# Three new planning margins and a longer one in a block-sparse attention and bilinear feed-forward kernel

## The chip, the cores and the metric

The kernel runs on one core of a Trainium2 chip. The metric is the device time in microseconds (us). The engines are TensorE (PE, with its weight loads PEld), VectorE (DVE), ScalarE (ACT), GpSimd (POOL) and SyncE (SP, which here only issues DMAs). All work in order: an instruction that waits holds up all that stand behind it on its engine.

## The reference

Four batches of eight heads attend over 768 positions of width 64. Positions are cut into 24 blocks of 32; a block of queries sees its neighbours, block 0, block 23 and three sampled blocks, and blocks 0 and 23 see everything:

```python
scores = scale * np.matmul(q, k.transpose(0, 1, 3, 2))
scores = np.where(mask, scores, -1000000000.0)
scores = scores - np.max(scores, axis=-1, keepdims=True)
attn = np.exp(scores)
attn = attn / (np.sum(attn, axis=-1, keepdims=True) + 1e-09)
x = np.matmul(attn, v)      # then heads side by side: 3072 rows of 512
out = ((x @ w_a) * (x @ w_b)) @ w_out   # 512 -> 1536 -> 512
```

Everything is float32; the kernel splits each operand into a high and a low float16 part, so that most products are three matmuls.

## The kernel before, in words

The attention goes by units, one block of queries of all heads: 96 units in 4 batches, 8 units to a chunk of 256 positions, 12 chunks. A sparse unit gathers its keys on POOL (lines 629 to 634, KG), computes scores on PE (L930, L1031), takes the maximum on DVE (L1046), exponentials on ACT (L1056), splits the weights (L948, L951, L955), turns them (on PE, L1109, for units 0 to 15; else by a DMA, L1081), and multiplies by gathered values (VG, loaded by SP at lines 656 to 669) on PE (L974). The sums go into xT (L1241, L1244). Eight finished units release one chunk of the feed-forward: 12 tiles of first products (L1273, "ab", 24 matmuls), their product on ACT and DVE (L1290 to L1305), 12 tiles of second products (L1333 to L1335).

A batch is prepared by `keys` and `values`: ACT's queue loads the raw tile (L493, L563), ACT takes its bound (L503, L571), POOL reduces it over partitions (L392), ACT and DVE make both halves (L508, L509; L583, L584). Keys are turned by PE in batch 0 (L541) and by a DMA in the others (L522); values are stored to memory (L588). `queries` loads a chunk's queries (L693), splits them (L704, L709, L711) and copies each half to the other partitions by a DMA (`turn_queries`, L735). The weights of the feed-forward come in 36 loads (L755), are rebuilt by DVE (L775 to L782) and split (L806 to L816); their raw tiles lie where the keys of batch 1 go later.

The order of all this is not written out. `Plan` keeps a clock of its own: each step of a flow yields an engine and a duration, and the plan takes next what can start first. An event carries the time at which it fired, and a flow that waits for it is not ready before. A plain number that is yielded moves a flow's ready time on by so much:

```python
if isinstance(got, int):
    self.ready += got
    value = self.ready
```

So a margin (LATE_Q, LATE_KS, LATE_VG and others) makes the plan believe that a DMA lands later. It adds no instruction and no wait to the program; it only moves what depends on that DMA, and with it everything else, to other places in the engines' orders. The rings of buffers are planned in the same way. Each DMA also takes one of eight landing counters in turn, whatever queue it is on, and its issuer waits until the DMA that had the counter before has landed; in the rows of the order below these are DMAHW0 to DMAHW7.

Of the kernel before, what the change touches and what calls it, by code (L numbers as in the profile page):

```python
# [53 lines left out]

LATE_PT, LATE_VG, LATE_AV, LATE_G = 2500, 2500, 1500, 700
LATE_S = 1000
LATE_HL, LATE_KS, LATE_Q = 2500, 2500, 2000
DMA_AHEAD = 1750
X_HIGH, X_UNITS = 600, 16

# [168 lines left out]
def dve(ns, fn):  # L229
    return [Way("DVE", ns, fn)]  # L230


def act(ns, fn):
    return [Way("ACT", ns, fn)]
# [6 lines left out]
def load_way(moved, fn):  # L241

    return [Way("LOAD", 475, fn, moved)]


def sp(ns, moved, fn):
    return [Way("SP", ns, fn, moved)]
# [3 lines left out]
def kernel(  # L251
# [41 lines left out]
    def take(tag, bufs):  # L293
        return rings.setdefault(tag, Ring(bufs)).take()
# [56 lines left out]
    v_stored = [Event(NG) for _ in range(B)]  # L351
    q_ready = [Event(3) for _ in range(NC)]
# [37 lines left out]
    def set_scale(a, floor=FLOOR):  # L390
        bits = power[:, a].bitcast(I32)
        yield pool(480, lambda: nc.gpsimd.partition_all_reduce(  # L392
            power[:, a], bound[:, a], P, bass_isa.ReduceOp.absmax
        ))
        yield dve(150, lambda: nc.vector.tensor_scalar(
            bits, bits, 0x7F800000, None, ALU.bitwise_and
        ))
        yield dve(150, lambda: nc.vector.tensor_scalar(
            rscale[:, a], power[:, a], floor, float(2.0 ** -14), ALU.max, ALU.mult
        ))  # L400
        end = yield dve(160, lambda: nc.vector.reciprocal(scale[:, a], rscale[:, a]))
        return end
# [67 lines left out]
    def gate(i):  # L470
        if i >= 0:
            yield s_sent[units[i]]

    def raw_tile(b, g, n):

        if b == 0:
            late = wab[:, NF // 2 :].rearrange("p f i a c x -> p (f i a c x)").bitcast(F32)
            late = late.rearrange("p (g x) -> p g x", x=2 * NT * D)
            return late[:, n * NG + g], parked
        yield w_freed  # L480
        t = stage[:, raw_taken[0] % RAW_BUFS]
        raw_taken[0] += 1
        freed = yield from take("raw", RAW_BUFS)
        return t, freed
# [5 lines left out]
    def keys(b, g):  # L490
        yield from gate(first_of[b] - GATE_KV)
        raw, freed = yield from raw_tile(b, g, 0)
        yield load_way(1000, lambda: nc.scalar.dma_start(raw, k[b, g]))  # L493
        if g + 1 < NG:
            plan.start(keys(b, g + 1), first_of[b] - LEAD_K)
        elif b > 0:
            plan.start(values(b, 0), first_of[b] - LEAD_V)
        t = raw.rearrange("p (t d) -> p t d", d=D)
        done = yield from take("ks", KS_BUFS)
        ks = work.tile([P, 2 * NT, P], F16, tag="ks", name=f"ks{b}_{g}", bufs=KS_BUFS)  # L500
        at = at_k + b * NG + g
        s = scale[:, at : at + 1]
        yield act(1020, lambda: nc.scalar.activation(  # L503
            ks[:, :, :D], t, AF.Abs, accum_out=bound[:, at : at + 1]
        ))
        end = yield from set_scale(slice(at, at + 1), FLOOR_QK)
        k_scale[b].fire(end)
        yield act(930, lambda: nc.scalar.activation(ks[:, :, :D], t, AF.Copy, scale=s))  # L508
        end = yield dve(1070, lambda: nc.vector.scalar_tensor_tensor(  # L509
            ks[:, :, D:], t, s, ks[:, :, :D], ALU.mult, ALU.subtract  # L510
        ))
        freed.fire(end)
        if b == 0:
            ends = Event(2)
            for h in range(2):
                plan.start(turn_keys(g, h, ks, ends, done), first_of[b] - LEAD_K, end)
            return
        if b == 1:
            yield w_freed
        if b >= 2:  # L520
            yield k_free[b - 2]
        end = yield sp(1700, 2200, lambda: nc.sync.dma_start_transpose(  # L522
            keysT[b % 2][:, 2 * g : 2 * g + 2, :].rearrange("p h (t s) -> p (h t) s", s=P),
            ks.rearrange("p t d -> p (t d)"),
        ))
        done.fire(end + LATE_KS)
        k_ready[b].fire(end + LATE_KS)
# [31 lines left out]
    def values(b, g):  # L559

        yield from gate(first_of[b] - GATE_KV)
        raw, freed = yield from raw_tile(b, g, 1)
        yield load_way(1000, lambda: nc.scalar.dma_start(raw, v[b, g]))  # L563
        if g + 1 < NG:
            plan.start(values(b, g + 1), first_of[b] - LEAD_V)
        elif b + 1 < B:
            plan.start(keys(b + 1, 0), first_of[b + 1] - LEAD_K)
        t = raw.rearrange("p (t x) -> p t x", t=NT)
        done = yield from take("ks", KS_BUFS)
        spare = work.tile([P, 2 * NT, P], F16, tag="ks", name=f"va{b}_{g}", bufs=KS_BUFS)  # L570
        end = yield act(1020, lambda: nc.scalar.activation(  # L571
            spare[:, :NT], t, AF.Abs,
            accum_out=bound_v[:, b * NG + g : b * NG + g + 1],
        ))
        done.fire(end)
        v_bound[b].fire(end)
        if g == NG - 1:
            plan.start(values_scale(b), first_of[b] - LEAD_V)
        yield v_scale[b]
        done = yield from take("ks", KS_BUFS)  # L580
        vs = work.tile([P, NT, 2, 2 * D], F16, tag="ks", name=f"vs{b}_{g}", bufs=KS_BUFS)
        s = scale[:, at_v + b : at_v + b + 1]
        yield act(930, lambda: nc.scalar.activation(vs[:, :, 0], t, AF.Copy, scale=s))  # L583
        end = yield dve(1015, lambda: nc.vector.scalar_tensor_tensor(  # L584
            vs[:, :, 1], t, s, vs[:, :, 0], ALU.mult, ALU.subtract
        ))
        freed.fire(end)
        end = yield sp(650, 1350, lambda: nc.sync.dma_start(  # L588
            vd[b][:, g * 4 * D : (g + 1) * 4 * D].rearrange("(t p) x -> p t x", p=P),
            vs.rearrange("p t a x -> p t (a x)"),  # L590
        ))
        done.fire(end)
        v_stored[b].fire(end)

    def values_scale(b):
        yield v_bound[b]
        at = at_v + b
        yield dve(150, lambda: nc.vector.reduce_max(
            bound[:, at : at + 1], bound_v[:, b * NG : (b + 1) * NG],
            axis=mybir.AxisListType.X,  # L600
        ))
        end = yield from set_scale(slice(at, at + 1))
        v_scale[b].fire(end)
# [79 lines left out]
    def queries(cc):  # L683
# [29 lines left out]
        ))  # L713
        freed.fire(end)
        plan.start(turn_queries(cc, 1), u0 - LEAD_Q, end)
        yield k_scale[b]

# [15 lines left out]
    def turn_queries(cc, a):  # L733

        end = yield sp(650, 700, lambda: nc.sync.dma_start(  # L735
            QT[cc][D:, 1 - a], QT[cc][:D, a]
        ))
        q_ready[cc].fire(end)


    def raw_weights(n, count):
# [722 lines left out]
```

## Time and profile before

| what | value |
|---|---|
| median of 3 runs | 862.08 us (860.63 to 865.51) |
| the profiled execution's own time | 856.35 us |
| its span, first to last instruction | 854.6 us |
| PE busy | 763.1 us, 89% |
| DVE busy | 587.0 us, 69% |
| ACT busy | 501.3 us, 59% |

Up to about 160 us the weights and the first batch are prepared while the first two chunks are attended to: DVE is nearly always busy there and PE is not. After it PE is busy nearly all the time, and from about 713 us on only feed-forward tiles are left. The page gives busy time over the whole span; the rows below are from views of single stretches.

### The profile page before, as it was taken

Reading aid. Unit: us, or ns where it says so; the run is one execution under the profiler, and the core shown is the slowest. Engines: PE = TensorE matmul, PEld = TensorE weight load, DVE = VectorE, ACT = ScalarE, POOL = GpSimd, SP = SyncE. Lnnn points to the kernel's source line nnn. Section 1 sums busy time; section 2 is a strip of 40 time slices with the busy share of each in tenths; the row PEclk is TensorE's granted clock in tenths of the full one; section 3 lists DMA queues with packets and bytes.
Section 4 is the critical chain, followed back from the end, with each engine's and each line's share of the span. In section 5 each row is a group of like instructions: output and inputs, shape, how many; then the busy total and the mean of one; then the engine's idle time right before and its main releaser. Section 6 shows DMA issues by size and latency. Waiting matters only on the chain.

```text
span 854.6 us, 24181 instructions
## 1 busy us (share of the span) xinstructions
PE 763.1 (89%) x9192; PEld 568.3 (66%) x9192; DVE 587.0 (69%) x1589; ACT 501.3 (59%) x1158; POOL 179.5 (21%) x428
## 2 busy tenths in 40 slices
PE   2256478799999979999999999999999999999998
PEld 1134366577767757767777867777777677777775
DVE  4999989998687568775677786755767876332222
ACT  6688779776675467684475765843845663232222
POOL 0642332300043133120034240200422310000000
PEclk9985589999999999999999999999999999999999
DMA  8767795577957589987676989667677767500000
GB/s 270 227 192 238 237 237 183 156 145 180 203 150 173 123 189 236 187 191 174 151 184 150 177 208 226 149 180 165 158 164 152 146 147 150 129 25 2 26 1 25
DMA packets 187758, 136.89 MB, mean 160 GB/s; under 512 B 130681, under 2 KB 155258, under 8 KB 187642
## 3 DMA queue, kind: packets, MB, share of 16 engines
q1 hardware_dynamic: 175712, 97.56, 51.7%
q10 hardware_dynamic: 11930, 37.79, 14.5%
q8 instruction: 72, 1.18, 0.6%
q14 instruction: 44, 0.36, 0.1%
HBM read 86.28 MB, written 12.58 MB: 116 GB/s over the span
## 4 chain that ended last, share of the span: by engine, by line
PE 62%; DVE 16%; DMA 9%; ACT 6%; issue 3%; SPq 2%; POOL 1%; ACTq 0%; POOLq 0%; DVEq 0%
PE ab L1273 33%; PE av L974 7%; PE o L1333 6%; PE o L1335 6%; PE o L1334 5%; PE s L930 4%; DMA VG<-vd 3%; DVE hl L955 2%; ACT sm L1056 2%; DMA keysT<-ks 2%; DVE xT L1244 2%; DVE low L1046 1%; DVE QT L711 1%; ACT QT L709 1%; PE s L1031 1%
## 5 line engine op out<-in xcount | busy, mean ns | idle before, releaser
L1273 PE MATMUL ab<-xT,wab 128*128 128x256 f16 x3456 | 403.8, 274 | 2.4 <-DVE a L1293 1.8
L1273 PEld LDWEIGHTS <-wab 128*128 128x128 f16 x3456 | 336.2, 98 | 67.8 <-issue 10.2
L1293 DVE SCALAR_TENSOR_TENSOR a<-a,to_g,ab 128x256 f32<-128x256 f32 x144 | 68.7, 478 | 116.5 <-ACT a L1290 115.0
L1290 ACT ACTIVATE a<-ab,w 128x256 f32<-128x256 f32 x144 | 67.3, 468 | 128.0 <-PE ab L1273 126.5
L1056 ACT ACTIVATE sm<-s,low,cq 128x256 f32<-128x256 f32 x176 | 97.8, 558 | 49.1 <-DVE low L1049 25.4
L629 POOL COPY KG<-keysT 128x384 int32<-128x384 int32 x88 | 57.0, 647 | 308.0 <-PE s L930 279.7
L974 PEld LDWEIGHTS <-VG 128*128 128x128 f16 x2688 | 99.2, 101 | 29.5 <-issue 20.2
L974 PE MATMUL av<-pt,VG 128*128 128x64 f16 x2688 | 105.4, 197 | 15.0 <-ACT pt L1115 6.9
L1333 PE MATMUL o<-woh,gh 128*128 128x512 f16 x288 | 109.7, 381 | 2.4 <-ACT gh L1302 2.4
L1335 PE MATMUL o<-wos,gl 128*128 128x512 f16 x288 | 109.2, 379 | 2.8 <-DVE gl L1305 2.8
L1334 PE MATMUL o<-wol,gh 128*128 128x512 f16 x288 | 109.2, 379 | 0.0
L955 DVE SCALAR_TENSOR_TENSOR hl<-sm,den,hl 128x256 f16<-128x256 f32 (+1 forms) x208 | 104.6, 510 | 3.3 <-ACT hl L948 1.5
L634 POOL COPY KG<-keysT 128x128 int32 x264 | 92.0, 385 | 45.2 <-issue 23.3
L1302 ACT ACTIVATE gh<-a 128x256 f16<-128x256 f32 x144 | 59.4, 413 | 57.6 <-DVE a L1293 55.0
L1305 DVE SCALAR_TENSOR_TENSOR gl<-gh,a 128x256 f16<-128x256 f16 x144 | 63.0, 438 | 29.7 <-ACT gh L1302 28.4
L1244 DVE SCALAR_TENSOR_TENSOR xT<-av,xT 64x256 f16<-64x256 f32 x96 | 40.4, 421 | 40.9 <-ACT xT L1241 40.1
L930 PE MATMUL s<-KG,QT 128*32 128x256 f16 x1408 | 59.6, 293 | 9.3 <-POOL KG L634 7.5
L1046 DVE TENSOR_REDUCE low<-s 128x2 f32<-128x512 f32 x88 | 60.0, 683 | 8.3 <-PE s L930 7.6
L1241 ACT ACTIVATE xT<-av 64x256 f16<-64x256 f32 x96 | 36.1, 376 | 42.5 <-PE av L974 41.3
L930 PEld LDWEIGHTS <-QT 128*32 128x32 f16 x1664 | 43.8, 102 | 18.2 <-issue 7.7
L1335 PEld LDWEIGHTS <-gl 128*128 128x128 f16 x288 | 28.1, 98 | 39.7 <-DVE gl L1305 6.9
L948 ACT ACTIVATE hl<-sm,den 128x256 f16<-128x256 f32 (+1 forms) x86 | 43.9, 514 | 9.9 <-DMA pt<-hl 2.5
(116 smaller groups left out, 771.7 us busy)
## 6 DMA issues: line engine op xcount, KB each, us to landing
VG<-vd SPq DMA_DIRECT2D x284, 64.0 KB, 2.3
VG<-vd SPq DMA_DIRECT2D x88, 192.0 KB, 3.1
VG<-vd SPq DMA_DIRECT2D x32, 384.0 KB, 3.7
q<-in_q_dram ACTq DMA_DIRECT2D x24, 256.0 KB, 5.1
QT<-QT SPq DMA_DIRECT2D x24, 256.0 KB, 3.3
vd<-vs SPq DMA_DIRECT2D x16, 384.0 KB, 3.1
out_dram<-ou SPq DMA_DIRECT2D x24, 256.0 KB, 2.3
stage<-in_k_dram ACTq DMA_DIRECT2D x12, 384.0 KB, 4.4
```

The lines of the kernel that those rows point to most:

```text
L634: nc.gpsimd.tensor_copy(to[:, :, (5 + r) * w : (6 + r) * w], of[:, :, bass.ds(at, w)])
L930: mm(to[h * BLK : (h + 1) * BLK], q_block(cc, i, 4 * hq + h, a), rhs(4 * hq + h), start=(first and a == 0), stop=(a == 1), skip_group_chec ...
L955: t = yield dve(221 + n * 1.03, lambda: nc.vector.scalar_tensor_tensor(lo, sm, over, hi, ALU.mult, ALU.subtract))
L974: mm(av[:, g, i % 2, :], w, pt[:, y, cols], start=(i % 2 == 0 and g == 0 and first and n + m == 0), stop=(last and n == len(terms) - 1 and ...
L1046: yield dve(685, lambda: nc.vector.tensor_reduce(mx, ps, axis=mybir.AxisListType.X, op=ALU.max, negate=True))
L1056: t = yield act(750, lambda hq=hq: nc.scalar.activation(sm[:, hq], ps[:, hq], AF.Exp, bias=low[:, at, hq, 0:1], scale=cq[:, cc, hq : hq + ...
L1273: mm(ab[:, i, :], wab[:, f, i, part, kt, :], xc[:, kt, a, :], start=(i == 0 and kt == 0 and part + a == 0), stop=(kt == KT - 1 and a == 1) ...
L1290: yield act(470, lambda: nc.scalar.activation(a_sb, ab[:, 0, :], AF.Copy, scale=w3[:, f : f + 1]))
L1293: t = yield dve(420, lambda: nc.vector.scalar_tensor_tensor(a_sb, a_sb, to_g[:, n : n + 1], ab[:, 1, :], ALU.mult, ALU.mult))
L1333: mm(po, gh[:, js], woh[:, f, :], start=(f == lo), stop=False)
L1334: mm(po, gh[:, js], wol[:, f, :], start=False, stop=False)
L1335: mm(po, gl[:, js], wos[:, f, :], start=False, stop=(f == hi - 1))
```

## The change

```diff
-LATE_HL, LATE_KS, LATE_Q = 2500, 2500, 2000
+LATE_HL, LATE_KS, LATE_Q = 2500, 4000, 2000
+LATE_KV, LATE_VD, LATE_QT = 1500, 2000, 1000
```
```diff
         yield load_way(1000, lambda: nc.scalar.dma_start(raw, k[b, g]))
+        yield LATE_KV
```
```diff
         yield load_way(1000, lambda: nc.scalar.dma_start(raw, v[b, g]))
+        yield LATE_KV
```
```diff
-        done.fire(end)
-        v_stored[b].fire(end)
+        done.fire(end + LATE_VD)
+        v_stored[b].fire(end + LATE_VD)
```
```diff
-        q_ready[cc].fire(end)
+        q_ready[cc].fire(end + LATE_QT)
```

After the change, the plan counts a raw tile of keys or values as there 1.5 us later, turned keys (and the buffer that they are turned from) 4.0 us after the transfer's end instead of 2.5, stored values (and their buffer) 2.0 us later, and turned queries 1.0 us later. Three lines are added, so that all line numbers behind line 57 are 1 to 3 higher in the changed kernel.

Nearly every engine's order changes from its first rows on. Three places matter below. The first is POOL at the start: the partition reductions (ISA power<-bound; 128x1 for keys, queries and values, 128x2 for a weight) and the first gather of keys (KG0). Before:

```order
L392 ISA power_93<-bound_91 128x1 [waits Activation_49] x5
L629 COPY KG0_84<-keysT0_78 128x8x48 [waits DVE_49,Activation_49]
L631 COPY KG0_84<-keysT0_78 128x8x16
L632 COPY KG0_84<-keysT0_78 128x8x16
L609 TENSOR_LOAD offs_k_110 [waits DVE_49]
```

After:

```order
L393 ISA power_93<-bound_91 128x1 [waits Activation_49] x5
L393 ISA power_93<-bound_91 128x1 [waits DVE_49]
L836 ISA power_93<-bound_91 128x2 [waits Activation_49]
L632 COPY KG0_84<-keysT0_78 128x8x48
L634 COPY KG0_84<-keysT0_78 128x8x16
L635 COPY KG0_84<-keysT0_78 128x8x16
```

The reductions of the values' bound and of the first weights' bound now stand ahead of the first gather of keys. On ACT, the load of the table of sampled blocks (L421) has moved from ahead of the first weight load to behind the bound of the first weights (L806); on DVE, the building of the mask (L448 to L463) has moved from ahead of the first weights' rebuilding to behind it, and three value halves (L584) from behind the first maximum of scores (L1046) to ahead of it.

The second is ACT where units 9 to 12 and the first tile of the feed-forward meet (sm: exponentials of a unit, hl: its split weights, QT2: the queries of the third chunk, stage: raw weights). Before:

```order
L948 ACTIVATE hl10_1418<-sm10_1376,den_98 128x256 [waits DMAHW1_49,DVE_49]
L755 DMA stage_77<-in_moe_w_b_dram 128x1024 [waits DMAHW3_49]
L1056 ACTIVATE sm11_1495,den_98<-s11_1372,low_97,cq_96 128x256 [waits DVE_49,PE_49]
L1056 ACTIVATE sm11_1495,den_98<-s11_1372,low_97,cq_96 128x256
L704 ACTIVATE QT2_1441,bound_91<-q2_1406 64x2048 [waits DMAHW7_49,DMAHW4_49]
L1056 ACTIVATE sm12_1539,den_98<-s12_1405,low_97,cq_96 128x256 [waits DVE_49,PE_49,Activation_49]
```

After:

```order
L1059 ACTIVATE sm11_1487,den_98<-s11_1367,low_97,cq_96 128x256 [waits DVE_49,PE_49]
L951 ACTIVATE hl10_1442<-sm10_1369,den_98 128x256 [waits DMAHW0_49,Activation_49]
L1059 ACTIVATE sm11_1487,den_98<-s11_1367,low_97,cq_96 128x256
L707 ACTIVATE QT2_1417,bound_91<-q2_1399 64x2048 [waits DMAHW3_49,DMAHW1_49]
L758 DMA stage_77<-in_moe_w_b_dram 128x1024 [waits DMAHW2_49]
L951 ACTIVATE hl10_1442<-sm10_1369,den_98 128x256 [waits Activation_49]
L1059 ACTIVATE sm12_1493,den_98<-s12_1398,low_97,cq_96 128x256 [waits DVE_49,PE_49,Activation_49]
```

The load of raw weights has moved behind both exponentials of unit 11 and the bound of the queries; the counter that it waits for is in both orders that of the same transfer, the load of values into VG1 for the dense unit 8.

The third is ACT where batch 3 is prepared, beside the feed-forward's chunk 6 (a6, gh6: its tiles; ks3, va3: keys and values of batch 3; q9: the queries of chunk 9). Before:

```order
L503 ACTIVATE ks3_3_9752,bound_91<-stage_77 128x12x64
L563 DMA stage_77<-in_v_dram 128x768
L508 ACTIVATE ks3_3_9752<-stage_77,scale_94 128x12x64
L693 DMA q9_9650<-in_q_dram 64x1024 x2
L571 ACTIVATE va3_0_9901,bound_v_92<-stage_77 128x768
L1290 ACTIVATE a6_3_9977<-ab6_3_9831,w3_99 128x256
L1302 ACTIVATE gh6_3_10023<-a6_3_9977 128x256
```

After:

```order
L696 DMA q9_9597<-in_q_dram 64x1024 x2
L505 ACTIVATE ks3_3_9780,bound_91<-stage_77 128x12x64
L1293 ACTIVATE a6_3_9937<-ab6_3_9854,w3_99 128x256
L1305 ACTIVATE gh6_3_9974<-a6_3_9937 128x256
L510 ACTIVATE ks3_3_9780<-stage_77,scale_94 128x12x64
L707 ACTIVATE QT9_9944,bound_91<-q9_9597 64x2048
L1293 ACTIVATE a6_4_10010<-ab6_4_9938,w3_99 128x256
```

The load of queries stands ahead of the last keys, and tile 3 of the feed-forward ahead of the values. Its second half takes over its counter from a turn of keys (L522) before, and from a load of raw values or keys (stage) now.

## Rows read from the trace of the kernel before

**Rows 1.** The page, part 1: busy us, share of the span, instructions.
```profile
PE 763.1 (89%) x9192; PEld 568.3 (66%) x9192; DVE 587.0 (69%) x1589; ACT 501.3 (59%) x1158; POOL 179.5 (21%) x428
```

**Rows 2.** Busy time by stage; columns: stretch, length, PE, PEld, DVE, ACT, POOL.
```profile
0.00:160.00 160.00, 85.38 (x1156) 63.19 (x1160) 140.39 (x347) 123.74 (x251) 53.64 (x102) 0.83 0.72 216
20.00:160.00 140.00, 80.89 (x1120) 59.45 (x1124) 132.45 (x313) 111.99 (x233) 51.67 (x93) 0.81 0.70 209
160.00:851.00 691.00, 677.70 (x8041) 505.07 (x8040) 446.12 (x1242) 377.58 (x907) 125.90 (x326) 1.00 0.66 147
300.00:320.00 20.00, 15.65 (x238) 11.15 (x235) 13.33 (x39) 13.59 (x31) 6.89 (x20) 0.91 0.89 193
```

**Rows 3.** DVE's groups by line and shape: busy us, mean ns, idle before.
```profile
L711 DVE SCALAR_TENSOR_TENSOR QT<-q,scale,QT 64x2048 f16<-64x2048 f32 x12 | 28.1, 2342 | 12.9 <-ACT QT L709 12.9
...
L584 DVE SCALAR_TENSOR_TENSOR vs<-wab,scale,vs 128x768 f16<-128x768 f32 x4 | 4.0, 1038 | 0.0
```

**Rows 4.** The timeline from 0 to 60 us: start, length, engine, what.
```profile
18.39 0.15 DVE L448 COPY mbox<-mbox 24x5 f32<-24x5 f32 x1
...
20.91 0.28 DVE L463 CAST mrows<-mbox 24x256 bf16<-24x256 f32 x1
...
27.32 1.29 POOL L629 COPY KG<-keysT 128x384 int32<-128x384 int32 x1 [9.03 <-ACT keysT L549]
...
29.02 2.13 POOL L634 COPY KG<-keysT 128x128 int32 x3
...
31.57 0.19 ACT L806 ACTIVATION_READ_ACCUMULATOR woh<-w 128x1 f32 x1
...
34.39 0.67 DVE L1046 TENSOR_REDUCE low<-s 128x2 f32<-128x512 f32 x1
```

**Rows 5.** ACT's timeline from 96 to 125 us.
```profile
105.78 1.13 ACTq L693 DMA_DIRECT2D q<-in_q_dram  x2
...
108.51 0.89 ACT L948 ACTIVATE hl<-sm,den 128x256 f16<-128x256 f32 x2
114.33 0.35 ACTq L755 DMA_DIRECT2D stage<-in_moe_w_b_dram  x1
114.79 0.56 ACT L1056 ACTIVATE sm<-s,low,cq 128x256 f32<-128x256 f32 x1 [5.39 <-DMA VG<-vd]
...
115.88 1.90 ACT L704 ACTIVATE QT<-q 64x2048 f16<-64x2048 f32 x1
```

**Rows 6.** The chain of waits in order of time: start, length, what.
```profile
106.68 7.63 DMA VG<-vd
```

**Rows 7.** DVE's timeline from 60 to 165 us.
```profile
116.02 0.17 DVE L1061 TENSOR_SCALAR den<-den 128x2 f32<-128x2 f32 x1 [3.56 <-ACT sm L1056]
```

**Rows 8.** ACT's timeline, batches 2 (352 to 369 us) and 3 (515 to 535 us).
```profile
363.62 0.84 ACT L571 ACTIVATE va<-stage 128x768 f16<-128x768 f32 x1 [3.06 <-DMA keysT<-ks]
...
525.40 4.18 ACTq L693 DMA_DIRECT2D q<-in_q_dram  x2
529.63 0.84 ACT L571 ACTIVATE va<-stage 128x768 f16<-128x768 f32 x1 [3.32 <-DMA keysT<-ks]
```

**Rows 9.** PE's timeline at three of its waits.
```profile
364.92 0.39 PE L1333 MATMUL o<-woh,gh 128*128 128x512 f16 x1 [0.48 <-ACT gh L1302]
...
531.50 2.78 PE L1273 MATMUL ab<-xT,wab 128*128 128x256 f16 x24 [1.22 <-DVE a L1293]
...
671.68 0.62 PE L930 MATMUL s<-KG,QT 128*32 128x256 f16 x16 [1.28 <-DMA QT<-QT]
```

## The prediction

> **What bounds the kernel now.** I read the page first: PE is busy for 763.1 us of 854.6, DVE for 587.0 [rows 1]. A mean over the whole span hides that there are two stages, so the second view is the busy time by stage [rows 2]. Up to 160 us PE works 85.38 us and DVE 140.39; between 20 and 160 us DVE stands still for 140 - 132.45 = 7.55 us in all. That stage is DVE's. From 160 to 851 us PE works 677.70 of 691 us at a full clock, so only 13.3 us are idle, and 4.35 of them fall into the 20 us from 300 on. That stage is PE's, and its work does not change. A change of order can therefore win or lose in two ways only: DVE's waits in the first stage, and PE's waits in the second. The third step was to follow the waits of ACT, DVE and PE in the timelines to what ended them.
>
> **The change, part by part.** No instruction is added to the program for a margin; the plan believes in later landings and deals the same work out anew. So the first question is whether the order puts more DVE work ahead of the feed-forward, which is what PE lives on. Counted in the two orders, ahead of DVE's product of the first feed-forward tile stand 250 instructions before and 258 now, ahead of the 12th 431 and 435, ahead of the 24th 545 and 547, of some 1590 in all. At 587.0 / 1589 = 0.37 us each [rows 1] that is 3.0, 1.5 and 0.7 us. Most of the first difference is one query half of 2.34 us [rows 3] that is now done sooner and had to be done anyway. By the 24th tile PE has sent the scores of units 0 to 24 in both orders, and from tile 9 of chunk 4 to the end of chunk 5 PE's two orders are the same. So the load of the first stage is the same within a microsecond, and I put nothing down for it. What is left are waits, each worked out by itself.
>
> *The start, +1.0.* The first gather of keys began on POOL at 27.32, when the last keys were copied, ended at 29.02 + 2.13 = 31.15, and DVE took the first maximum at 34.39 [rows 4]. Now two reductions stand ahead of it on POOL, and the later one needs the bound of the first output weights, which ACT had at 31.57 + 0.19 = 31.76 [rows 4]. The building of the mask, 18.39 to 21.19 on DVE [rows 4], now stands behind those weights, so that they may come up to 2.8 us earlier. The gather thus starts at 28.96 to 31.76, which is 1.6 to 4.4 us late, and unit 0 with it. The cover is DVE's own work: the mask fills the time in which DVE would wait for the gather, and three value halves of 1.04 us [rows 3], 3.1 us together, have moved ahead of that first maximum. That covers all but 1.3 us of the longest delay. If the cover holds, this costs nothing; if it is gone, 4.4 us. The 1.3 us are nearest, and I take 1.0.
>
> *The held-up load of weights, -2.0.* From 108.51 + 0.89 = 109.40 to 114.79 ACT did nothing [rows 5]. It stood at the issue of a weight load, whose landing counter was last used by a load of values that was issued at 106.68 and landed 7.63 us later [rows 6]. Behind it stood unit 11's exponentials, for which DVE waited 3.56 us [rows 7]: the largest of DVE's waits after 20 us. The load still waits for the same transfer, but two exponentials, one split and the queries' bound have moved ahead of it: 2 x 0.75 + 0.45 + 2.1 = 4.0 us of ACT's work (from the rows at 114.79, 108.51 and 115.88, the read-out of the sum at 0.19 counted with each [rows 5]). That leaves 5.39 - 4.0 = 1.4 us of the wait, and behind it the second half of a split. DVE's gain lies between 0, if the queries (issued at 105.78 [rows 5]) have not landed when their bound is due and ACT waits for them instead, and 3.56. I take the middle.
>
> *The turn of keys in batches 2 and 3, -1.5.* In batch 3 the issue of the query loads held ACT from 525.40 to 529.58, until a turn of keys had landed [rows 8]; the feed-forward's tile stood behind it, and PE waited 1.22 us [rows 9]. The second half of these loads now waits for the counter of a raw load that was issued eight DMAs sooner, and one feed-forward tile has moved ahead of the values: this wait should go, between 0 and -1.22, and I take -1.2. In batch 2 the bound of the values waited 3.06 us for a buffer that a turn of keys was still read from [rows 8], and PE lost 0.48 us [rows 9]. The four bounds now stand farther apart, between tiles 7 and 10 of chunk 3: 0 to -0.48, I take -0.3. No wait takes their place nearby that I can see: ACT works for only 377.58 of the 691 us [rows 2].
>
> *The turned queries, -0.6.* The longest wait of PE for turned queries was 1.28 us at 671.68, at the first unit of chunk 11 [rows 9]. Its scores now stand behind the values of the unit before, which came after them; that hides some of it. Between 0 and -1.28 I take the middle.
>
> *What stays.* The 4.35 us from 300 to 320 [rows 2] are waits at the end of chunk 2 for the values and the xT of units 29 to 31. There the orders differ only in that one unit's scores stand behind two tiles instead of ahead of them. No margin touches these values. I take 0.
>
> The sum is +1.0 - 2.0 - 1.5 - 0.6 = -3.1 us against the profiled execution's 856.35 us, 854.6 of it span. The median of the runs shown is 862.08, which is 5.7 us above that execution; on the median the sum gives 859.0 us.
>
> **The rivals.** *All waits are cured.* The margins are put on the transfers behind which ACT and PE were seen waiting, for 3.32 and 3.06 us on ACT [rows 8]. If every term above reaches its far end and the start is covered: -3.56 - 1.70 - 1.28 = -6.5, or 855.5 us. Against it: two of the three depend on a landing that is as late as it was.
>
> *The waits only move.* A wait sits at the issue, and whatever then stands behind it is held up: in the 5.39 us at 109.40 it was the exponentials, and now it is others [rows 5]. The margins lengthen what the consumer of a transfer expects, but the plan's account of the eight landing counters gets none of them. If each wait removed comes back at another load, the sum is 0, and the time 862 us. The Trainium skill speaks for this rival: by "DMA: Bandwidth & Descriptors", section "Anatomy of one DMA — SWDGE (gpsimd) path", a transfer never waits for a semaphore on the DMA engines, the wait is served by the engine that issues it, before it goes out. The trace agrees, with ACT idle for 5.39 us at an issue [rows 5].
>
> *The start is late and stays late.* This is the one on the slower side. POOL's reduction of the first weights' bound holds up the first gather, and the table of sampled blocks, whose load now goes out after the first weights' bound, holds up the last three copies of it. Price: the 4.4 us above and the 2.13 us of these copies [rows 4], 6.5 us of DVE standing still, with nothing won elsewhere in the first stage: 868.6 us. It decides if DVE's waits between 20 and 160 us grow from 7.55 to over 12 us. For it speaks that DVE has little slack there; against it that 3.1 us of its work have moved ahead.
>
> **How the numbers follow.** Less than about 0.5% (4.3 us) can't be told from no change here. I give my forecast, -3.1 us, 0.40; its own range is 855 to 862.5, so that half of it lies beyond the limit of 857.8 us and half within. All waits cured: 0.20, faster. The waits only move: 0.18, no change. A late start: 0.22, slower. That makes faster 0.20 + 0.20 = 0.40, same 0.20 + 0.18 = 0.38, slower 0.22. For the range I go from the cured case with some of the 4.35 us at 300 on top, 851, to the late start, 869.
>
> **What the changed profile would show.** The start: POOL's first gather at 29 to 32 us, and DVE's idle time between 20 and 160 us at about 6 us; over 12 would make the slower rival right. The load of weights: an idle time of ACT of under 2 us before the second half of unit 10's split. Batch 3: no wait of PE of over 0.5 us at tile 5 of chunk 6. Chunk 11: a wait for turned queries of under 1 us. If PE's idle time from 160 us to the last matmul is still 13 us or more and DVE's 7 us, the waits have only moved. The forecast is wrong if a new wait of over 4 us stands in either stage, at a place that none of these rows shows.

## The result: 1.1% slower, and what the profile after shows

The changed kernel took 871.62 us (median of 4 runs, 866.47 to 878.61), the kernel before 863.63 us in the same comparison (4 runs, 860.63 to 865.51). The ratio is 1.0111, with a 95% interval of 1.0061 to 1.016: slower by some 8 us, where 859.0 was forecast and 869 was the upper end. Here and below a ratio leaves out executions over 1.5% above the fastest of the same kernel, so that it isn't the quotient of the two medians. The profiled execution of the changed kernel is one of 872.88 us.

The page, part 1, of the changed kernel, which answers to [rows 1]:

```profile
PE 770.3 (88%) x9192; PEld 572.1 (66%) x9192; DVE 585.0 (67%) x1591; ACT 502.7 (58%) x1156; POOL 182.0 (21%) x428
```

PE executes the same 9192 instructions, yet is busy for 7.2 us longer. Nothing was added to its work; part of it ran at a lower granted clock. The busy time by stage (stretch, length, then PE, PEld, DVE, ACT, POOL, the granted clock, DMA) answers to [rows 2]:

```profile
0.00:160.00 160.00, 85.18 (x1142) 63.89 (x1143) 137.40 (x345) 125.62 (x253) 56.68 (x106) 0.84 0.74 218
20.00:160.00 140.00, 80.84 (x1106) 60.15 (x1107) 130.39 (x322) 112.88 (x233) 54.72 (x97) 0.82 0.73 211
160.00:868.00 708.00, 685.17 (x8050) 508.19 (x8049) 447.56 (x1247) 377.09 (x904) 125.30 (x322) 0.99 0.64 143
300.00:320.00 20.00, 16.65 (x253) 11.62 (x252) 12.88 (x38) 12.56 (x31) 4.40 (x13) 1.00 0.62 136
```

DVE stands still for 140 - 130.39 = 9.61 us between 20 and 160 us, 2.1 more than before, and PE for 708 - 685.17 = 22.8 us from 160 us on, 9.5 more. The two stretches in which PE is furthest behind the first profile are 160 to 240 and 300 to 340 us. First the kernel before, then the changed one:

```profile
160.00:240.00 80.00, 79.15 (x904) 59.50 (x904) 66.03 (x180) 55.91 (x124) 10.08 (x28) 0.99 0.80 179
300.00:340.00 40.00, 34.86 (x494) 25.94 (x491) 31.03 (x94) 28.30 (x69) 14.30 (x35) 0.96 1.00 218
```
```profile
160.00:240.00 80.00, 75.48 (x846) 55.49 (x846) 65.62 (x176) 54.76 (x121) 9.28 (x21) 0.98 0.76 172
300.00:340.00 40.00, 33.36 (x436) 23.56 (x435) 27.25 (x79) 23.67 (x57) 11.28 (x27) 0.87 0.70 159
```

That is 3.67 and 1.50 us of PE's busy time, and in the second the clock is lower as well.

**The start.** The timeline of the changed kernel, all engines, which answers to [rows 4]:

```profile
26.57 0.48 ACTq L422 DMA_DIRECT2D mrow<-in_sampled_blocks_dram  x1
...
30.91 0.61 POOL L836 PARTITION_ALL_REDUCE power<-bound  x1 [3.09 <-ACT woh L809]
31.39 0.57 POOL L632 COPY KG<-keysT 128x384 int32<-128x384 int32 x1
...
32.13 2.86 DVE L587 SCALAR_TENSOR_TENSOR vs<-wab,scale,vs 128x768 f16<-128x768 f32 x3
34.92 0.26 DVE L449 COPY mbox<-mbox 24x5 f32<-24x5 f32 x1
...
37.93 0.28 DVE L464 CAST mrows<-mbox 24x256 bf16<-24x256 f32 x1
...
38.27 0.35 PE L1034 MATMUL s<-mrows,ident 128*32 128x192 bf16 x4 [14.53 <-DVE mrows L464]
...
40.28 0.67 DVE L1049 TENSOR_REDUCE low<-s 128x2 f32<-128x512 f32 x1
...
42.72 6.61 POOL L632 COPY KG<-keysT 128x384 int32<-128x384 int32 x1
...
50.09 1.04 PE L933 MATMUL s<-KG,QT 128*32 128x256 f16 x16 [4.49 <-POOL KG L637]
```

POOL's first gather begins at 31.39, within the 29 to 32 that was forecast. But the first maximum comes at 40.28, 5.9 us later than in [rows 4] and 4.6 later than in a second profile of before (kernel 12 below), and not because of the gather: the mask, built by 21.19 us before, is built from 34.92 to 38.21, behind the three value halves of 2.86 us that were to cover the delay, and PE waits for it. The large copy of a later unit's gather then takes 6.61 us, where that of the first took 0.57, and PE waits for that too. The feed-forward begins late too. PE's timelines of before, of its second profile and of the changed kernel, the first tile of the feed-forward in each:

```profile
108.33 3.74 PE L1273 MATMUL ab<-xT,wab 128*128 128x256 f16 x24
```
```profile
109.67 2.87 PE L1273 MATMUL ab<-xT,wab 128*128 128x256 f16 x24
```
```profile
114.65 5.19 PE L1276 MATMUL ab<-xT,wab 128*128 128x256 f16 x24
```

The changed kernel is 6.3 and 5.0 us behind the two at its first tile and 8.0 and 5.2 behind at its 25th. At the end of the span it is 16.5 and 7.1 us behind.

**The waits that were to go.** ACT's and DVE's timelines around 109 to 118 us answer to [rows 5, 7]:

```profile
116.77 0.33 ACTq L758 DMA_DIRECT2D stage<-in_moe_w_b_dram  x1
117.16 0.51 ACT L951 ACTIVATE hl<-sm,den 128x256 f16<-128x256 f32 x1 [1.69 <-DMA VG<-vd]
```
```profile
117.70 0.48 DVE L958 SCALAR_TENSOR_TENSOR hl<-sm,den,hl 128x256 f16<-128x256 f32 x1 [1.38 <-ACT hl L951]
```

ACT's 5.39 us have become 1.69, DVE's 3.56 have become 1.38, as forecast, although the transfer behind which the load stands is as slow as in [rows 6] (7.83 us). The query loads of batch 3, which held ACT in [rows 8], and the first scores of chunk 11 and tile 5 of chunk 6 on PE [rows 9] no longer wait:

```profile
537.43 0.48 ACTq L696 DMA_DIRECT2D q<-in_q_dram  x1
...
538.90 0.47 ACTq L696 DMA_DIRECT2D q<-in_q_dram  x1
```
```profile
547.74 2.46 PE L1276 MATMUL ab<-xT,wab 128*128 128x256 f16 x21
...
686.42 0.61 PE L933 MATMUL s<-KG,QT 128*32 128x256 f16 x16
```

PE's timeline of the changed kernel shows what it waits for instead; each row's idle time stands in brackets:

```profile
201.40 0.79 PE L977 MATMUL av<-pt,VG 128*128 128x64 f16 x21 [1.35 <-DMA VG<-vd]
...
317.96 0.88 PE L977 MATMUL av<-pt,VG 128*128 128x64 f16 x24 [2.10 <-DMA pt<-hl]
320.26 0.27 PE L1034 MATMUL s<-mrows,ident 128*32 128x192 bf16 x4 [1.42 <-ACT sm L1059]
...
323.05 1.28 PE L977 MATMUL av<-pt,VG 128*128 128x64 f16 x21 [1.87 <-DMA VG<-vd]
...
535.35 0.95 PE L977 MATMUL av<-pt,VG 128*128 128x64 f16 x24 [2.15 <-DMA pt<-hl]
...
666.12 0.90 PE L977 MATMUL av<-pt,VG 128*128 128x64 f16 x24 [1.54 <-DMA pt<-hl]
...
690.10 0.88 PE L977 MATMUL av<-pt,VG 128*128 128x64 f16 x24 [1.04 <-DMA pt<-hl]
```

All but the one for exponentials (ACT sm) are waits for weights turned by a DMA and for gathered values, two transfers whose margins the change leaves alone.

### The profile page after: what moved, and what is told of

Same layout as the page of the kernel before. It is cut to its first block, busy times and chain, and to the rows that moved or that the text cites. A ratio compares the mean times of both kernels' runs of the same rounds, so it can differ in the third digit from the quotient of the medians.

```text
span 871.1 us, 24194 instructions
## 1 busy us (share of the span) xinstructions
PE 770.3 (88%) x9192; PEld 572.1 (66%) x9192; DVE 585.0 (67%) x1591; ACT 502.7 (58%) x1156; POOL 182.0 (21%) x428
## 4 chain that ended last, share of the span: by engine, by line
PE 61%; DVE 15%; DMA 10%; ACT 6%; issue 3%; SPq 3%; POOL 1%; ACTq 1%; POOLq 0%; DVEq 0%
PE ab L1276 33%; PE av L977 6%; PE o L1336 6%; PE o L1338 5%; PE o L1337 5%; PE s L933 3%; DMA pt<-hl 3%; DMA VG<-vd 3%; DVE hl L958 2%; DVE xT L1247 2%; DMA q<-in_q_dram 1%; DVE low L1049 1%; ACT sm L1059 1%; DMA keysT<-in_moe_w_out_dram 1%; ACT xT L1244 1%
## 5 line engine op out<-in xcount | busy, mean ns | idle before, releaser
L977 PE MATMUL av<-pt,VG 128*128 128x64 f16 x2688 | 107.6, 198 | 25.0 <-DMA pt<-hl 9.1
L977 PEld LDWEIGHTS <-VG 128*128 128x128 f16 x2688 | 101.2, 102 | 43.3 <-issue 26.9
L632 POOL COPY KG<-keysT 128x384 int32<-128x384 int32 x88 | 63.3, 720 | 275.0 <-PE s L933 262.5
L1034 PE MATMUL s<-mrows,ident 128*32 128x192 bf16 (+1 forms) x352 | 26.0, 284 | 34.7 <-ACT sm L1059 15.5
```

The lines of the kernel that those rows point to most:

```text
L977: mm(av[:, g, i % 2, :], w, pt[:, y, cols], start=(i % 2 == 0 and g == 0 and first and n + m == 0), stop=(last and n == len(terms) - 1 and ...
```

## The experiments

All are comparisons with the kernel before, measured on the same chip beside it. Three theories at first. Theory 1: the margins of batch 0 make the start late, and that costs. Theory 2: the later margins cost. Theory 3: it is not the margins but that the order is dealt anew.

| kernel | median, us | ratio to before | 95% interval | PE busy 160:240 | PE busy 300:340 |
|---|---|---|---|---|---|
| before, first and second profile | 862.5 | 1 | | 79.15, 78.59 | 34.86, 35.11 |
| changed | 871.62 | 1.0111 | 1.0061 to 1.016 | 75.48 | 33.36 |
| 1 not in batch 0 | 871.91 | 1.0102 | 1.0066 to 1.0138 | 79.45 | 27.65 |
| 2 loads' margin in batch 0 only | 865.51 | 1.0032 | 0.9991 to 1.0073 | 69.43 | 36.69 |
| 3 turned keys only | 868.11 | 1.0073 | 1.0037 to 1.011 | 79.45 | 33.31 |
| 4 stored values only | 860.05 | 0.995 | 0.9914 to 0.9986 | 72.33 | 34.70 |
| 5 turned keys, batch 1 only | 870.15 | 1.0094 | 1.005 to 1.0139 | 79.23 | 32.93 |
| 6 turned keys, batches 2 and 3 | 861.92 | 1.0017 | 0.9975 to 1.0058 | 79.45 | 33.61 |
| 7 control, queries 2050 | 865.55 | 1.0051 | 1.0015 to 1.0087 | 79.31 | 35.09 |
| 8 changed, not in batch 1 | 871.27 | 1.0153 | 1.0102 to 1.0203 | 73.85 | 38.07 |
| 9 turned keys 3250, batch 1 | 862.99 | 1.0022 | 0.9988 to 1.0057 | | |
| 10 turned keys 1000, batch 1 | 869.13 | 1.0094 | 1.0058 to 1.013 | 79.21 | 33.00 |
| 11 batches 2 and 3 only | 862.80 | 1.0018 | 0.9984 to 1.0053 | 79.45 | 34.31 |
| 12 before, again | 866.20 | 1.0046 | 1.0003 to 1.009 | 78.59 | 35.11 |
| 13 as 10, gate 1 sooner | 870.54 | 1.0076 | 1.0043 to 1.0109 | 79.45 | 33.49 |
| 14 before, gate 2 later | 871.83 | 1.0119 | 1.0063 to 1.0176 | 79.45 | 36.19 |
| 15 before, gate 2 sooner | 867.31 | 1.0064 | 1.0022 to 1.0106 | 78.44 | 34.78 |
| 16 changed, gate 2 sooner | 876.68 | 1.0158 | 1.0105 to 1.0211 | 74.96 | 30.08 |
| 17 control, scores 1050 | 866.75 | 1.0046 | 1.0004 to 1.0087 | 77.80 | 35.68 |
| 18 control, scores 950 | 868.10 | 1.0043 | 1.0006 to 1.0079 | 75.15 | 34.30 |

The runs came in five sets; the median of before lay between 861.25 and 864.79 us in them, and the first row shows that of kernels 1 to 4. The changed kernel's own row is of the four runs above. Kernels 8, 14 and 16 were run 6 times each, the others 8 to 12 times. The last two columns, in us, are of the one execution of each kernel that was profiled, and that can lie far from the median: for kernels 10, 13 and 14 it was the fastest of all (863.26, 861.22 and 865.11 us), for 2, 16 and 18 one of the slowest (870.21, 883.02 and 871.97). The busy times of kernel 9, whose profiled execution was its slowest (871.82), are left out.

### 1 to 4: one part at a time

Kernel 1, against the changed kernel:

```diff
-        yield LATE_KV
+        yield LATE_KV if b > 0 else 0
-        done.fire(end + LATE_VD)
+        done.fire(end + (LATE_VD if b > 0 else 0))      # and v_stored
-        q_ready[cc].fire(end + LATE_QT)
+        q_ready[cc].fire(end + (LATE_QT if cc > 0 else 0))
```

> All four margins as in the changed kernel, but none in batch 0 and none for the first chunk's queries, so that the first 280 or so of ACT's instructions are in the order of before; the later margins stand. Theory 1, the loss comes from the start (the first feed-forward chunk is handed over 7.8 us late): about 861 to 865 us, within 0.5% of before, and the 12th feed-forward tile within 1.5 us of where it starts before. Theory 2, the later margins cost it: 868 us or more, with PE's new waits behind 240 us as in the changed kernel. Theory 3, any new deal of the order costs some per cent in either direction: no fixed value, anything from 858 to 872.

Kernels 2, 3 and 4 keep one margin each and set the others as before (`yield LATE_KV if b == 0 else 0` and nothing else; `LATE_KS` 4000 and nothing else; `LATE_VD` and nothing else).

> Only the margin of 1500 ns on the loads of keys and values of batch 0; every other margin as before. Theory 1 (the start): 869 to 873 us, with the first maximum on DVE near 40 us and the first feed-forward tile 5 us or more later than before. Theory 2 (the later margins): 862 to 865 us, the late start made good by the 12th tile.

> Only the longer margin of the transposed keys, 4000 ns for 2500; the order is that of before up to ACT's 299th instruction. Theory 1: 861 to 865 us. Theory 2: 866 us or more, with PE waits of over 1 us at the start of chunk 3 or in batches 2 and 3.

> Only the margin of 2000 ns on the stored values; the order is that of before up to ACT's 53rd instruction, so that the first gather of keys and the mask are as before. Theory 1 (it is the loads' margin at the start that costs): 861 to 865 us. Theory 2: 866 us or more. Should the time be above 866 with a late first feed-forward tile, the start is at fault, but by the stored values and not by the loads.

Measured: 1.0102, 1.0032, 1.0073 and 0.995. That speaks for theory 2, and theory 1 falls as the only cause: without any margin in batch 0 the kernel is as slow as with them. The loads' margin of batch 0 by itself costs little that can be told from nothing, although the trace of kernel 2 has PE lose 10 us between 160 and 240 us. But kernel 2 doesn't test the whole late start: its first maximum is late (at 41.5 us), its first feed-forward tile, expected 5 us or more later, is not (108.74 us). The late first tile is in the traces of kernels 8 and 16 below (115.05 and 114.02 us). Kernel 1's trace shows the start as before, and the loss at the boundary from chunk 2 to chunk 3:

```profile
160.00:240.00 80.00, 79.45 (x880) 59.63 (x873) 66.56 (x182) 54.25 (x122) 9.79 (x28) 0.98 0.77 182
300.00:340.00 40.00, 27.65 (x427) 20.92 (x425) 24.56 (x69) 20.74 (x51) 10.60 (x30) 0.79 0.78 163
```

There PE waits for the values of unit 30, and ACT for queries that were loaded 7 us later than before (at 308.21 us, before at 301.03):

```profile
317.55 2.74 PE L977 MATMUL av<-pt,VG 128*128 128x64 f16 x48 [6.20 <-DMA pt<-hl]
```
```profile
315.57 1.91 ACT L707 ACTIVATE QT<-q 64x2048 f16<-64x2048 f32 x1 [4.98 <-DMA q<-in_q_dram]
```

The margin of the stored values by itself, kernel 4, came out faster than both of its expectations and is the only one that is faster than before, by 0.5%; kernel 12 below says how little that is.

### 5, 6, 8 and 11: one batch at a time

Kernels 5 and 6 have nothing but the longer margin of turned keys, for one batch or for two:

```diff
-        done.fire(end + LATE_KS)
-        k_ready[b].fire(end + LATE_KS)
+        done.fire(end + (LATE_KS if b == 1 else 2500))      # kernel 6: if b > 1
+        k_ready[b].fire(end + (LATE_KS if b == 1 else 2500))
```

> The longer margin of transposed keys (4000 ns) for batch 1 alone, nothing else changed. In PE's order the scores of units 24 and 25 stand 2.6 and 9.1 us of PE's own work later than before, while the values of unit 31 keep their place, 0.7 us of work ahead of chunk 3's first feed-forward tile. Theory 2a (the margin hands batch 1's units out later, and they are late where PE has nothing else to do, at the boundary from chunk 2 to 3): 866 to 869 us, all of the 5.6 us that the margin costs in all batches, and PE idle between 300 and 340 us 3 to 5 us longer than before. Theory 2b (the loss is in batches 2 and 3): 861 to 864 us.

> The longer margin of transposed keys for batches 2 and 3 alone; the order is that of before up to ACT's 430th instruction, so that the boundary at 300 to 340 us is as before. Theory 2a: 861 to 864 us. Theory 2b: 866 to 869 us.

Kernel 8 is the changed kernel with its margins set as before for `b == 1`; kernel 11 the changed kernel with them for `b > 1` only. The margin of the turned queries stands in both.

> The changed kernel without its margins on the loads, the stored values and the transposed keys of batch 1; those of the other batches and of the turned queries stand. Theory 2a: 864 to 868 us, 3 to 6 less than the changed kernel, with 5 us or less of PE waits between 300 and 340 us. Theory 1 (the start) and theory 2b (batches 2 and 3): 869 to 873 us, no better than the changed kernel.

> The changed kernel with its margins on loads, stored values and transposed keys in batches 2 and 3 only (and those of the turned queries). The order is that of before up to ACT's 388th instruction, past the boundary at 315 us. With it the four combinations of the start's margins and batch 1's are there: both 871, batch 1's without the start's 872, the start's without batch 1's 871. If each of the two is enough by itself to make unit 31 late, and together they cost no more than one: 861 to 866 us. If the loss sits in batches 2 and 3: 869 to 873 us.

Measured: 1.0094, 1.0017, 1.0153 and 1.0018. So the margins of batches 2 and 3, on which half of my forecast's gain stood, cost and win nothing that can be measured, and the kernel with that of batch 1's turned keys alone is 0.9% slower. The four combinations are there: neither the start's margins nor batch 1's, 1.0018; the start's alone, 1.0153; batch 1's alone, 1.0102; both, 1.0111. Each is enough without the other, and together they cost no more than one; each of the four was measured in another set. Kernel 8 missed its expectation of 864 to 868: the boundary is good, as theory 2a had it, and the loss is at 160 to 240 us instead:

```profile
160.00:240.00 80.00, 73.85 (x814) 54.63 (x811) 61.75 (x163) 50.20 (x110) 7.82 (x17) 0.94 0.79 168
300.00:340.00 40.00, 38.07 (x509) 28.07 (x507) 28.74 (x86) 25.92 (x63) 10.72 (x28) 0.96 0.77 178
```

### 9 and 10: the size of one margin

Batch 1's turned keys again, as in kernel 5, but with 3250 ns, and with 1000 ns, which is less than before. The two orders take kernel 5's apart: one has its late scores of units 24 and 25, the other its order behind them.

> The margin of batch 1's transposed keys 3250 ns for 2500, nothing else. The order changes in one place only: the scores of units 24, 25 and 28 stand 2.6, 10.4 and 5.2 us of PE's work later; from the scores of unit 38 on PE's order is that of before. Theory 2a (late scores of batch 1's first units come out as waits of PE at the boundary from chunk 2 to 3): 866 to 870 us. Theory 2c (what costs is the new order behind that boundary): 861 to 864 us.

> The margin of batch 1's transposed keys 1000 ns for 2500, nothing else. Units 24 and 25 stand 1.3 us of PE's work earlier than before, but behind the boundary, from the scores of unit 38 on, the order is the one of the kernel with 4000 ns for batch 1, which took 870.15. Theory 2a: 860 to 864 us. Theory 2c: 867 to 871 us.

Measured: 1.0022 with 3250 ns, 1.0094 with 1000 ns. Both are as theory 2c expected (862.99 and 869.13 us). Theory 2a falls: late scores of batch 1's first units cost nothing that can be measured. And a margin that is shorter than before by 1500 ns costs as much as one that is longer by 1500 ns (1.0094 in kernel 5). By the traces PE's order is the same in kernels 5 and 10 from about 310 us on, and in kernel 9 it is that of before from about 300 us on. What the margin says of the landing is not what costs here; the order that the plan comes to behind the boundary costs.

### 13 to 16: a gate, and the order behind it

In six kernels that were slower, the first load of batch 2's keys went out at 324.92 us or later, in all others before 319. The next four move that load by itself, through the gate that lets it in; in kernel 10 it stands at 326.07.

```diff
     def keys(b, g):
-        yield from gate(first_of[b] - GATE_KV)
+        yield from gate(first_of[b] - GATE_KV - (2 if b == 2 else 0))
```

(Kernel 13: 1, on kernel 10; kernel 14: -2, kernel 15: 2, both on before; kernel 16: 2, on the changed kernel.)

> The kernel with 1000 ns for batch 1's transposed keys (869.13), and the first loads of keys and values of batch 2 let in one unit sooner. Behind 345 us of PE's work the order stays that kernel's. Theory 2d (what costs is that batch 2's eight loads go out 8 us or more later, which the trace has at 326.07 us and later in every slow kernel but one, at 324.92 in that one, and before 319 in every other): 861 to 865 us, the first such load before 322 us. Theory 2e (the order behind 400 us, in which units 71 to 95 stand 5.2 to 7.8 us of PE's work later than before): 867 to 871 us.

> The kernel before, with batch 2's loads let in two units later; nothing else. The order is that of before up to the first of them, ACT's 385th instruction, and behind 345 us of PE's work it is that of the kernel with 1000 ns. Theory 2d: 867 to 871 us, with the first load at 325 us or later. Theory 2e: 867 to 871 us as well; the two part at the next kernel.

> The kernel before, with batch 2's loads let in two units sooner; nothing else. Behind 345 us of PE's work the order is again that of the kernel with 1000 ns. Theory 2d: 858 to 863 us, the first load at 310 to 315 us. Theory 2e: 867 to 871 us.

> The changed kernel, with batch 2's loads let in two units sooner; its start and its margins stand. Theory 2d, with the start costing only by way of late loads: 861 to 865 us. Theory 1 (the late start costs by itself) or theory 2e without its units 71 to 95 (this order has them 2.6 to 3.9 us sooner than before): 868 to 873 us.

The loads did move. ACT's timelines of kernels 13, 14, 15 and 16, one row of each:

```profile
310.18 0.34 ACTq L494 DMA_DIRECT2D stage<-in_k_dram  x1
```
```profile
329.24 0.33 ACTq L494 DMA_DIRECT2D stage<-in_k_dram  x1
```
```profile
306.38 0.33 ACTq L494 DMA_DIRECT2D stage<-in_k_dram  x1
```
```profile
317.31 0.33 ACTq L494 DMA_DIRECT2D stage<-in_k_dram  x1
```

The times did not follow: 1.0076, 1.0119, 1.0064 and 1.0158. By the medians alone, with before at 864.79 us in that set, it is 1.0066, 1.0081, 1.0029 and 1.0137. Theory 2d falls; a neat separation of 14 kernels by one number was no cause. Kernel 16, at 876.68 us, is slower than either theory expected, and nothing here explains it.

Theory 2e keeps standing for kernels 5, 10, 13 and 15, which share an order behind 345 us of PE's work, and for kernel 14 in part: in the traces its order on PE becomes that of kernel 10 only at about 580 us, so that they share the late units 71 to 95 and little ahead of them. All five are slower, by 0.64 to 1.19%, kernel 15 hardly more than the unchanged kernel below. Units 71 to 95 aren't the changed kernel's cause: in kernel 16, the slowest of all, they stand sooner than before, and in the changed kernel's trace some stand sooner and some later.

### 7, 17, 18 and 12: what any new order costs, and what none costs

Three controls change a margin that the change leaves alone by 50 ns (`LATE_Q` 2050; `LATE_S` 1050; `LATE_S` 950). Kernel 12 is the kernel before, unchanged.

> A control: none of the four margins; the margin on the queries' loads, which the change leaves alone, is 2050 ns for 2000. That is no better or worse an estimate of the landing, but the order differs from before in some 300 of ACT's 871 instructions, from the 159th on. Theory 3 (any new deal of the order moves the time, whatever the margin says): more than 3 us from before in either direction, 856 to 872. Theory 2a: units 24 and 25 stand 1.3 us of work earlier than before and unit 31's values where they were, so 860 to 865 us.

> A control: none of the change, but the margin on the reading of scores, which the change leaves alone, 1050 ns for 1000. The order differs from before in some 400 of ACT's 871 instructions, from the 61st on. Theory 3 (a new deal of the order is slower than this kernel's by itself, 0.7% in the mean of those measured so far): 865 to 871 us. Rival (the loss belongs to what the margins move; a new deal without a meaning is neutral): 860 to 865 us.

> The same control the other way, 950 ns for 1000; some 400 of ACT's instructions stand elsewhere, from the 87th on. Theory 3: 865 to 871 us, slower although the margin goes the other way. Rival: 860 to 865 us. If one of the two is faster than before and one slower, the deal is noise around before, and theory 3 falls too.

> The kernel before, unchanged, for a second profile of it: its first one was of 856.35 us, 6 below the median. It tells which of the differences in PE's lost time between the two profiled executions are the change's, and which only one execution's. Expected: the lost time up to 300 us the same within 1 us, a boundary at 300 to 320 us with 4 to 6 us of waits, and the rest of the difference behind 320 us.

The controls came out at 1.0051, 1.0046 and 1.0043, the unchanged kernel at 1.0046. Theory 3 expected 865 to 871 us for kernels 17 and 18 and got 866.75 and 868.10. But the unchanged kernel was as far off as they, so that a new order costing something by itself isn't shown. What is shown is the size below which a ratio tells nothing here: about 0.5%, with 8 to 12 runs against 23 to 35. The changed kernel lies 1.0111 - 1.0047 (the mean of the controls) = 0.64% above that, about 5.5 us, if its own comparison is off by as much as theirs, which isn't shown.

Kernel 12's second profile of the same program is the other finding. Its execution took 865.80 us, 9.45 more than the first. The busy time from 340 to 360 us, first profile, then second:

```profile
340.00:360.00 20.00, 20.00 (x265) 14.95 (x261) 13.99 (x39) 14.37 (x32) 4.52 (x14) 1.00 0.94 192
```
```profile
340.00:360.00 20.00, 17.09 (x209) 11.62 (x208) 12.03 (x35) 10.18 (x29) 5.06 (x16) 0.91 1.14 186
```

One and the same order has PE busy throughout in one execution and idle for 2.91 us, at a lower clock, in the next; in the second its longest wait there is for gathered values:

```profile
355.81 1.28 PE L974 MATMUL av<-pt,VG 128*128 128x64 f16 x21 [1.41 <-DMA VG<-vd]
```

My expectation for it, that the two would agree up to 300 us, was a miss as well: PE is busy for 79.04 us between 20 and 160 us, against 80.89 [rows 2], and its clock there is 0.87 against 0.81. The waits at 300 to 320 us, 4.89 us, are within the 4 to 6 expected.

## Why the prediction was wrong, point by point

**The method of the sum.** The step that failed is "What is left are waits, each worked out by itself". Waits of 1.2 to 5.4 us were read in one execution, each was taken away, and what the new order would wait for elsewhere was put at nothing ("No wait takes their place nearby that I can see"). They went, as the two orders said. Most of them were real, for the second profile of before has them again: ACT's at the held-up load, and PE's at tile 5 of chunk 6 and for the queries of chunk 11 (ACT's and PE's timelines; only the 0.48 us of batch 2 are missing):

```profile
116.21 0.56 ACT L1056 ACTIVATE sm<-s,low,cq 128x256 f32<-128x256 f32 x1 [5.22 <-DMA VG<-vd]
```
```profile
542.46 2.78 PE L1273 MATMUL ab<-xT,wab 128*128 128x256 f16 x24 [1.78 <-DVE a L1293]
...
681.69 0.62 PE L930 MATMUL s<-KG,QT 128*32 128x256 f16 x16 [0.94 <-DMA QT<-QT]
```

What failed is the nothing put down for new waits: PE's idle time from 160 us on still grew from 13.3 us (16.75 in the second profile of before) to 22.8, mostly at places that stand in none of the rows. The plan deals every engine's order anew, and the new order has waits of its own. Terms of 0.3 to 2 us can't be added up for such a change, and the one execution that I read, of 856.35 us, was faster than most and had fewer waits than the second.

**The start, +1.0.** Its size was wrong, and so was its cover. I had let the first weights come up to 2.8 us earlier, and the mask and the value halves fill the time. But unit 0's scores need the mask, which I had counted as cover only, and in the trace the halves stand ahead of it: PE waits for the mask, and unit 0's first maximum is 5.9 us late against the first profile and 4.6 against the second, beyond my upper bound of 4.4. DVE's idle time doesn't show this, since DVE was at work on other things. PE's first feed-forward tile is 5.0 to 6.3 us late, and at 160 to 240 us PE is busy for 3.67 us less than in the first profile of before and 3.11 less than in the second.

**The held-up load, -2.0.** Right in its place and near in size, though the middle of 0 to 3.56 is 1.8 and not 2.0: ACT's wait went by 3.7 us, DVE's by 2.2. But nothing of it was won: DVE's idle time of 20 to 160 us, forecast at about 6 us, is 9.61, and PE is busy there for 80.84 us, before 80.89, and begins the feed-forward later.

**Turns of keys -1.5, turned queries -0.6.** The waits of 1.22 and 1.28 us are gone. That of batch 2, 0.48 us, became 0.74. In their place stand 2.15 us at 535.35 and 1.54 and 1.04 us at 666.12 and 690.10. Kernels 6 and 11, with the margins of batches 2 and 3 alone, bear out the sum of the two: nothing (1.0017, 1.0018).

**What stays, 300 to 320 us.** "No margin touches these values" was wrong: batch 1's margins move the units at this boundary and the queries of chunk 3. PE's busy time from 300 to 340 us fell from 34.86 to 33.36 us, and in kernel 1 to 27.65.

**What I left out.** A wait of PE was priced at its own length. From 320 to 340 us the granted clock of the changed kernel is 0.74 in the mean, so that PE ran for part of that stretch, about 321 to 331 us, at 1.2 GHz and not at 2.4, behind and between the three waits of 1.42 to 2.10 us above:

```profile
320.00:340.00 20.00, 16.71 (x183) 11.94 (x183) 14.37 (x41) 11.11 (x27) 6.88 (x14) 0.74 0.78 183
```

Over the whole program PE's busy time grew by 7.2 us against the first profile of before and by 4.1 against the second (766.2 us), with the same instructions.

**The rivals.** The late start named the side and nearly the size (868.6). The start is late, but not by the way that was given: its mark, DVE idle for more than 12 us, was not reached (9.61), and without it kernel 1 is as slow. That it came nearest is in part luck. That waits only move came nearest to what happened to batches 2 and 3. None had the boundary at 315 us, and none that a new order could be slower as a whole.

**What stays open.** That the margins of batch 0 and those of batch 1 are each enough for 1% or more, beside those of the later batches, and that both together cost no more, is what was measured (kernels 8, 1 and 11). Which wait carries it is not known. The late first tile is in the changed kernel and in kernels 8 and 16, three of the slower ones, and isn't ruled out as their cost; but kernel 1 is as slow without it, and kernel 17, whose first tile comes at 112.84 us, is only 0.5% slower. The two stretches in which the changed kernel's trace falls behind most, 3.1 to 3.7 and 1.5 to 1.8 us, come near the 5.5 us above the controls, but they don't carry over: kernel 14 does as well as before in both and is 1.2% slower, and kernel 18 loses 4.0 us in the first and is only 0.4% slower. Even that is weak, for kernel 14's trace is of its fastest execution and kernel 18's of one of its slowest. Two places were named and moved by themselves, units 24 and 25 and the first loads of batch 2, and neither was the cause. With one profile for each changed order, and executions of the kernel before between 853 and 873 us, a loss of 8 us can't be laid to a place by comparing traces.

## What to carry to other kernels

Where a change makes a planner deal a whole order anew, don't add up the waits that go: forecast about no change, with the slower side as wide as the faster, because the new order brings waits of its own that the old trace can't show. Before reading waits of 1 us out of a trace, take a second profile of the same kernel: what the two don't share is no term of a sum, and how far they lie apart (here 9.45 us) says how small a sum can be told at all. And test a margin in both directions and a meaningless one beside it, since a shorter and a longer one that cost the same, as here, speak against its size as the cause.

## What the runs showed of the hardware

The large copy of a gather on POOL, 0.72 us in the mean of the 88 in the changed kernel, was stretched to 6.61 us at 42.72, and in kernel 8, with the same order there, the three small copies of the same unit's gather took 6.55 us:

```profile
42.53 0.50 POOL L632 COPY KG<-keysT 128x384 int32<-128x384 int32 x1
42.98 6.55 POOL L637 COPY KG<-keysT 128x128 int32 x3
```

In both profiles of before the large copy took 1.29 us at most between 26 and 60 us. DVE meanwhile runs its weight steps and splits, most of the longer ones with two tensors as inputs, without a gap (DVE's timeline of the changed kernel, three of its rows):

```profile
45.90 0.67 DVE L785 SCALAR_TENSOR_TENSOR w<-stage,w 128x512 int32<-128x512 int32 x1
...
46.97 1.19 DVE L782 SCALAR_TENSOR_TENSOR wab<-stage,wab 128x1024 int32<-128x1024 int32 x1
48.09 0.86 DVE L958 SCALAR_TENSOR_TENSOR hl<-sm,den,hl 128x256 f16<-128x256 f32 x2
```

The Trainium skill, "SBUF — State Buffer", section "SBUF: two separate sides", says that DVE and GpSimd share a pair of ports under an exclusive lock, which a DVE instruction with two inputs in SBUF takes for its whole length against a GpSimd one that reads SBUF. The trace fits this, but POOL was held for 6 us, far longer than any one DVE instruction there (1.19 us at most), over a row in which some have one input only. In before DVE does work of the same kinds between 42 and 58 us, and no copy is held like this. That the lock is the reason isn't shown; no run here tests it by itself.
